# A conditioned attention and feed-forward block: token-major residual, crossbar transposes and resident output weights

## The chip, the cores and the metric

The kernel runs on one core of one Trainium2 chip. Times are device microseconds of that core. All times compared here are of runs in the fast state, beside runs of the kernel before on the same chip. The groups of runs ran on different chips; the kernel before took 1413.2 to 1414.2 us on each (median), so times are compared across groups too. Engines are named as in the profile: PE (TensorE matmuls), PEld (its weight loads), DVE (VectorE), ACT (ScalarE), POOL (GpSimd), SP (SyncE, which issues DMAs). In the kernels, SBUF tiles hold operands and PSUM banks (`ps`) the results of matmuls; a crossbar transpose is a DMA that transposes on its way (`dma_start_transpose`).

## The reference

```python
sa, ca, ga, sb, cb, gb = silu(c) @ w_mod            # six rows of 1024
h = layernorm(x) * (1 + ca) + sa                    # x: 2048 tokens x 1024
x = x + ga * attention(h)     # 32 query heads, 4 key heads, 512 cached keys, Dh 128, then @ wo (4096 x 1024)
h = layernorm(x) * (1 + cb) + sb
x = x + gb * ((silu(h @ w_gate) * (h @ w_up)) @ w_down)       # 3584 hidden columns
```

Both kernels work through chunks of 512 tokens. All four chunks pass attention and its output projection first, then all four pass the feed-forward. A chunk has 32 heads; a head costs 8 matmuls of 512 columns for the query, 4 for the scores, and 16 of 129 columns for probabilities times values (the last column sums the probabilities).

## The kernel before

The residual `xT` lies with features on partitions, so a layernorm sums over partitions. That is done on TensorE with a matrix of ones, twice a chunk and layernorm:

```python
for dt in range(DT):                                   # 8 matmuls; 8 more over the squares
    mm(bank(bS), ones_bf[:, :], xT[:, dt, chs], dt == 0, dt == DT - 1, ...)
```

Each normalised head is transposed on TensorE and copied out of PSUM by VectorE:

```python
def otr(i):
    for j in range(TPC):                               # 4 blocks of 128x128
        transpose(bb[:, j * P:(j + 1) * P], o_s[os_][:, j, :], [B_os[os_]], PB[TRB])
    T.op(DVE, lambda: V.tensor_copy(oT_all[:, h, :], bb[:, 0:CH]), ...)
```

The loop over heads (cut to its order); one pair of PSUM banks serves the whole down projection:

```python
for i in range(NA + 3):
    ...                         # query weights, 2 MB pieces of output weights, x tiles, late modulation
    qproj(i); scores(i - 1); pv(i - 2); otr(i - 3)
    if hD == Hq - 1: oproj_plain(chD)
    run_bg(...)                 # a step of a layernorm
DNB = [4, 5]                    # down projection: all pairs of output tiles use these two banks
```

Output weights are loaded again for each chunk. The later modulation rows come from 256 matmuls with one moving column. The result is transposed back on TensorE.

The softmax here doesn't subtract the row's maximum and nothing guards it: scores larger than these inputs give would overflow.

Of the kernel before, what the change touches and what calls it, by code (L numbers as in the profile page):

```python
# [3 lines left out]
ALU = mybir.AluOpType  # L4
AF = mybir.ActivationFunctionType
BF16 = mybir.dt.bfloat16
# [4 lines left out]
class _Stream:  # L11
    def __init__(self, name, sem, issuer, inc=1, self_exempt=False):
        self.name = name
        self.sem = sem
        self.issuer = issuer
        self.inc = inc
        self.count = 0
        self.self_exempt = self_exempt

# [20 lines left out]
class _Tracker:  # L40
    def __init__(self):
        self.issuer_synced = {}

    def stream(self, name, sem, issuer, inc=1, self_exempt=False):
        return _Stream(name, sem, issuer, inc, self_exempt)

    def _synced(self, st):
        key = id(st.issuer)
        d = self.issuer_synced.get(key)
        if d is None:  # L50
            d = {}
            self.issuer_synced[key] = d
        return d

    def op(self, st, emit, reads=(), writes=()):
        req = {}
        for b in reads:
            lw = b.last_write
            if lw is not None:
                s, c = lw  # L60
                if req.get(s, 0) < c:
                    req[s] = c
        for b in writes:
            lw = b.last_write
            if lw is not None:
                s, c = lw
                if req.get(s, 0) < c:
                    req[s] = c
            for s, c in b.reads.items():
                if req.get(s, 0) < c:  # L70
                    req[s] = c
        synced = self._synced(st)
        eng = st.issuer
        for s, c in req.items():
            if s is st and st.self_exempt:
                continue
            if synced.get(s, 0) >= c:
                continue
            eng.wait_ge(s.sem, c)
            synced[s] = c  # L80
        ins = emit()
        st.count += st.inc
        c = st.count
        ins.then_inc(st.sem, st.inc)
        for b in reads:
            b.reads[st] = c
        for b in writes:
            b.last_write = (st, c)
            b.reads = {}
        return c  # L90

    def wait_all(self, st, target):
        synced = self._synced(st)
        c = target.count
        if c > 0 and synced.get(target, 0) < c:
            st.issuer.wait_ge(target.sem, c)
            synced[target] = c


class _Arena:  # L100

    def __init__(self, tensor_ap, nbytes):
        self.t = tensor_ap
        self.nbytes = nbytes
        self.off = 0
        self.gen = 0
        self.regs = []

    def reset(self):
        self.off = 0  # L110
        self.gen += 1

    def take(self, shape_free, dtype, bufs):
        n = 1
        for s in shape_free:
            n *= s
        esz = 2 if dtype == BF16 else 4
        nb = n * esz
        nb_al = (nb + 63) // 64 * 64
        assert self.off + nb_al <= self.nbytes, "arena overflow"  # L120
        start, end = self.off, self.off + nb
        for (g, s0, e0, obufs) in self.regs:
            if g != self.gen and s0 < end and start < e0:
                for nbuf in bufs:
                    for ob in obufs:
                        nbuf.absorb(ob)
        self.regs.append((self.gen, start, end, list(bufs)))
        e0 = start // 2
        ap = self.t[:, e0:e0 + nb // 2]
        if dtype != BF16:  # L130
            ap = ap.bitcast(dtype)
        if len(shape_free) == 2:
            ap = ap.rearrange("p (a b) -> p a b", a=shape_free[0])
        elif len(shape_free) == 3:
            ap = ap.rearrange("p (a b c) -> p a b c", a=shape_free[0], b=shape_free[1])
        self.off += nb_al
        return ap


def bass_adaLN_cond__sliding_block_cached__swiglu_ffn__prompt_kernel(  # L140
# [16 lines left out]
    HD = A_wq.shape[1]  # L157
    Hq = HD // Dh
# [3 lines left out]
    assert Dh == P and D % P == 0 and S % 512 == 0 and W % P == 0  # L162
    DT = D // P
    ST = S // P
# [5 lines left out]
    NJ = 6 * DT  # L170
    assert NJ % 4 == 0 and Hq % 4 == 0 and FT % 4 == 0 and DT % 2 == 0 and Hq >= 8
    WMG = NJ // 4
    HG = Hq // 4
    FG = FT // 4
    GK = Hkv * KT
    assert GK <= 16
    att_scale = float(Dh) ** -0.5
    eps = 1e-5
    inv_d = 1.0 / float(D)
    NA = NCH * Hq  # L180
    NFI = NCH * FT
    DSTEPS = FT // 4
    assert DT // 2 * DSTEPS <= FT
    assert (DT // 2) * 8 <= Hq
# [5 lines left out]

    PE = T.stream("pe", nc.alloc_semaphore("s_pe"), nc.tensor, self_exempt=True)
    ACT = T.stream("act", nc.alloc_semaphore("s_act"), nc.scalar)
    DVE = T.stream("dve", nc.alloc_semaphore("s_dve"), nc.vector)
    POOL = T.stream("pool", nc.alloc_semaphore("s_pool"), nc.gpsimd)

    def dq(name, issuer=None):
        return T.stream(name, nc.alloc_semaphore(name), issuer or nc.sync, inc=16)

    S_ = lambda name, shape, dt: nc.alloc_sbuf_tensor(name, shape, dt)
    xT = S_("xT", [P, DT, S], BF16)  # L200
    hT = S_("hT", [P, DT, S], BF16)
    ident = S_("ident", [P, P], BF16)
    ones_bf = S_("ones_bf", [P, P], BF16)
    eps_col = S_("eps_col", [P, 1], F32)
    c6 = S_("c6", [P, NJ], F32)
    c6a = S_("c6a", [P, 2 * DT], F32)
    g1 = S_("g1", [P, DT], F32)
    g2 = S_("g2", [P, DT], F32)
    mod_bf = S_("mod_bf", [P, NJ], BF16)
    gtmp_bf = S_("gtmp_bf", [P, DT], BF16)  # L210
    cT_bf = S_("cT_bf", [P, DT], BF16)
    th_c = S_("th_c", [P, DT], F32)
    sg_c = S_("sg_c", [P, DT], F32)
    sc_bf = S_("sc_bf", [P, DT], BF16)
    rl = S_("rl", [P, 4], F32)
    xnat_t = S_("xnat", [P, 4, D], BF16)
    xnat = [xnat_t[:, i, :] for i in range(4)]
    ln_mean = S_("ln_mean", [P, CH], F32)
    ln_msq = S_("ln_msq", [P, CH], F32)
    ln_var = S_("ln_var", [P, CH], F32)  # L220
    ln_A = S_("ln_A", [P, CH], BF16)
    ln_B = S_("ln_B", [P, CH], BF16)
    NSQ = 8
    ln_sq = [S_("ln_sq%d" % i, [P, CH], BF16) for i in range(NSQ)]
    ln_t = [S_("ln_t%d" % i, [P, CH], BF16) for i in range(2)]
    ln_n = [S_("ln_n%d" % i, [P, CH], BF16) for i in range(2)]

    ARENA_BYTES = 108 * 1024
    arena_t = S_("arena", [P, ARENA_BYTES // 2], BF16)
    arena = _Arena(arena_t[:, :], ARENA_BYTES)  # L230

    ps_h = nc.alloc_psum_tensor("ps", [P, 4096], F32)
    ps = ps_h[:, :]
    ps_t = ps.tensor
# [7 lines left out]
    PB = [_Buf("bank%d" % b) for b in range(8)]  # L242

    B_xT = [[_Buf("xT_%d_%d" % (dt, ch)) for ch in range(NCH)] for dt in range(DT)]
    B_hT = [[_Buf("hT_%d_%d" % (dt, ch)) for ch in range(NCH)] for dt in range(DT)]
    B_ident = _Buf("ident"); B_ones = _Buf("ones"); B_eps = _Buf("eps")
    B_c6 = _Buf("c6"); B_c6a = _Buf("c6a"); B_g1 = _Buf("g1"); B_g2 = _Buf("g2")
    B_modbf = _Buf("modbf"); B_gtmp = _Buf("gtmp")
    B_cT = _Buf("cT"); B_thc = _Buf("thc"); B_sgc = _Buf("sgc"); B_sc = _Buf("sc")
    B_rl = _Buf("rl")  # L250
    B_xnat = [_Buf("xnat%d" % i) for i in range(4)]
    B_mean = _Buf("mean"); B_msq = _Buf("msq"); B_var = _Buf("var"); B_A = _Buf("A"); B_B = _Buf("B")
    B_sq = [_Buf("sq%d" % i) for i in range(NSQ)]
    B_lnt = [_Buf("lnt%d" % i) for i in range(2)]
    B_lnn = [_Buf("lnn%d" % i) for i in range(2)]

    Q_c = dq("q_c")
    Q_x = [dq("q_x%d" % i) for i in range(4)]
    Q_out = [dq("q_out%d" % i) for i in range(4)]

    QB = 4
    SCB = [0, 1, 2, 3]
    OA = 5
    OBT = 6
    TRB = 7
    OPB = 7
    OT_OFF = [0, 130, 260]
    MOD_EARLY_OFF = 0
    MOD_LATE_OFF = 400
    GB = [0, 1]  # L270
    UB = [2, 3]
    DNB = [4, 5]
    YTB = 6

    with nc.Block() as block:

        @block.gpsimd
        def _(g):
            V = nc.vector
            A = nc.scalar  # L280
            TE = nc.tensor
            SP = nc.sync

            def mm(out_ap, lhsT, rhs, start, stop, reads, bank_buf):
                T.op(PE, lambda: TE.matmul(out_ap, lhsT, rhs, start=start, stop=stop),  # L285
                     reads=reads, writes=[bank_buf])

            def transpose(out_ap, in_ap, reads, bank_buf):
                T.op(PE, lambda: TE.transpose(out_ap, in_ap, ident[:, :]),  # L289
                     reads=reads + [B_ident], writes=[bank_buf])  # L290
# [561 lines left out]
```

## Time and profile before

| | before |
|---|---|
| time, median of the first three runs | 1414.79 us |
| span of the profiled run | 1412.8 us |
| PE busy, share of span | 95% |
| DVE busy | 610.2 us |
| DMA moved | 178.53 MB |

These are lines of the profile's page of the kernel before: engines, the hardware DMA queue (packets, MB, share of 16 engines' time), and the chain of work that ended last.

```profile
span 1412.8 us, 20538 instructions
...
PE 1346.9 (95%) x8445; PEld 700.7 (50%) x8592; DVE 610.2 (43%) x1324; ACT 415.0 (29%) x674; POOL 59.4 (4%) x65
...
q1 hardware_dynamic: 237264, 177.22, 41.0%
...
PE 91%; DVE 3%; issue 2%; ACT 2%; SPq 2%; DMA 1%; DVEq 0%; ACTq 0%
...
L637 DVE COPY arena<-ps 128x512 bf16<-128x512 bf16 x128 | 53.1, 415 | 0.2 <-PE ps L289 0.2
L289 PE MATMUL ps<-ident,arena 128*128 128x128 bf16 x528 | 51.0, 221 | 1.4 <-DVE arena L637 1.4
```

The chain is 91% PE, so what counts is TensorE: work it need not do, and gaps between its matmuls. The mean of 221 ns for a transpose is a latency and not a cost, since matmuls overlap. A cost is read from start to start in the timeline: 216 ns for 512 columns, 59 for 129, 55 for a transpose. The busy share does not tell products from other work: 784 transposes and 128 sums over ones are inside those 95%.

The waits of PE in the kernel before (line waiting, what it waited for, total us, times, longest):

```profile
PE ps L285 <- DVE xT L776: 11.0, 24, 0.7
PE ps L289 <- DMA xnat<-in_A_x_dram: 7.6, 2, 4.7
PE ps L285 <- ACT hT L466: 6.4, 1, 6.4
PE ps L285 <- DVE arena L626: 6.4, 8, 1.0
PE ps L285 <- DVE arena L637: 6.2, 4, 1.7
```

L776 is the residual update of the down projection, L626 the scaling of a head, L637 the copy of a transposed head. The timeline of PE across a change of down columns shows what one of the first line's waits is (start, us, what, count, idle before it):

```profile
896.99 12.25 PE L285 MATMUL ps<-arena 128*128 128x512 bf16 x55
909.96 0.38 PE L285 MATMUL ps<-arena 128*128 128x512 bf16 x1 [0.72 <-DVE xT L776]
910.53 12.04 PE L285 MATMUL ps<-arena 128*128 128x512 bf16 x54 [0.19 <-DVE xT L776]
```

### The profile page before, as it was taken

Reading aid. Unit: us, or ns where it says so; the run is one execution under the profiler, and the core shown is the slowest. Engines: PE = TensorE matmul, PEld = TensorE weight load, DVE = VectorE, ACT = ScalarE, POOL = GpSimd, SP = SyncE. Lnnn points to the kernel's source line nnn. Section 1 sums busy time; section 2 is a strip of 40 time slices with the busy share of each in tenths; the row PEclk is TensorE's granted clock in tenths of the full one; section 3 lists DMA queues with packets and bytes.
Section 4 is the critical chain, followed back from the end, with each engine's and each line's share of the span. In section 5 each row is a group of like instructions: output and inputs, shape, how many; then the busy total and the mean of one; then the engine's idle time right before and its main releaser. Section 6 shows DMA issues by size and latency. Waiting matters only on the chain.

```text
span 1412.8 us, 20538 instructions
## 1 busy us (share of the span) xinstructions
PE 1346.9 (95%) x8445; PEld 700.7 (50%) x8592; DVE 610.2 (43%) x1324; ACT 415.0 (29%) x674; POOL 59.4 (4%) x65
## 2 busy tenths in 40 slices
PE   5989999999999999999999999999999999999998
PEld 3556644556545566455554444444443444444443
DVE  4566554656613566235671245313331333124311
ACT  4455540456503666025760021001110111001100
POOL 0220021000010000110001100000000000000000
PEclk7999999999999999999999999999999999999999
DMA  9663204522143421434204485308721683129410
GB/s 304 199 183 120 90 31 120 154 86 61 61 120 111 120 69 61 117 92 121 75 16 114 141 268 171 111 15 271 222 96 52 200 278 126 52 94 300 151 52 30
DMA packets 237357, 178.53 MB, mean 126 GB/s; under 512 B 7888, under 2 KB 233168, under 8 KB 237264
## 3 DMA queue, kind: packets, MB, share of 16 engines
q1 hardware_dynamic: 237264, 177.22, 41.0%
q8 instruction: 67, 1.10, 0.3%
q14 instruction: 26, 0.21, 0.1%
HBM read 173.02 MB, written 4.19 MB: 125 GB/s over the span
## 4 chain that ended last, share of the span: by engine, by line
PE 91%; DVE 3%; issue 2%; ACT 2%; SPq 2%; DMA 1%; DVEq 0%; ACTq 0%
PE ps L285 89%; PE ps L289 2%; ACT arena L603 1%; DVE xT L776 1%; DMA xnat<-in_A_x_dram 1%; DVE arena L626 1%; DVE rl L623 1%; SPq L526 0%; SPq L361 0%; ACT L603 0%; ACT L447 0%; DVE xnat L789 0%; SPq L530 0%; DVE ln_var L440 0%; DVE arena L628 0%
## 5 line engine op out<-in xcount | busy, mean ns | idle before, releaser
L285 PE MATMUL ps<-arena 128*128 128x512 bf16 (+1 forms) x4431 | 671.0, 306 | 17.4 <-DVE xT L776 11.0
L285 PE MATMUL ps<-hT,arena 128*128 128x512 bf16 x2724 | 618.6, 380 | 16.0 <-ACT hT L466 6.4
L285 PEld LDWEIGHTS ps<-arena 128*128 128x128 bf16 x4480 | 365.8, 98 | 339.3 <-issue 15.3
L285 PEld LDWEIGHTS ps<-hT,arena 128*128 128x128 bf16 x2816 | 270.5, 98 | 318.5 <-DMA arena<-in_A_wq_dram 6.3
L603 ACT ACTIVATE arena<-ps 128x512 bf16<-128x512 f32 x512 | 305.5, 597 | 347.0 <-PE ps L285 312.2
L756 ACT ACTIVATE arena<-ps 128x512 bf16<-128x512 f32 x112 | 66.9, 597 | 543.7 <-PE ps L285 543.7
L757 DVE SCALAR_TENSOR_TENSOR arena<-arena,ps 128x512 bf16<-128x512 bf16 x112 | 77.0, 688 | 173.5 <-ACT arena L756 173.5
L591 DVE CAST arena<-ps 128x512 bf16<-128x512 f32 x128 | 88.4, 690 | 49.8 <-PE ps L285 45.1
L776 DVE SCALAR_TENSOR_TENSOR xT<-ps,c,xT 128x512 bf16<-128x512 f32 x32 | 22.6, 747 | 183.2 <-PE ps L285 183.2
L760 DVE SCALAR_TENSOR_TENSOR arena<-arena,ps 128x512 bf16<-128x512 bf16 x112 | 77.0, 688 | 53.8 <-PE ps L285 53.7
L651 DVE SCALAR_TENSOR_TENSOR xT<-ps,c,xT 128x512 bf16<-128x512 f32 x32 | 24.0, 751 | 152.3 <-PE ps L285 152.1
L427 POOL TENSOR_TENSOR ln_sq<-xT 128x512 bf16<-128x512 bf16 x56 | 58.4, 1060 | 717.3 <-PE ps L285 671.8
L626 DVE TENSOR_TENSOR arena<-ps,rl 128x384 bf16<-128x384 f32 x128 | 71.4, 558 | 4.4
L622 DVE RECIPROCAL rl<-ps 128x3 f32<-128x3 f32 x128 | 23.1, 180 | 110.7 <-PE ps L285 110.7
L637 DVE COPY arena<-ps 128x512 bf16<-128x512 bf16 x128 | 53.1, 415 | 0.2 <-PE ps L289 0.2
L289 PE MATMUL ps<-ident,arena 128*128 128x128 bf16 x528 | 51.0, 221 | 1.4 <-DVE arena L637 1.4
L628 DVE TENSOR_SCALAR arena<-ps,rl 128x128 bf16<-128x128 f32 x128 | 44.9, 351 | 4.6
L289 PEld LDWEIGHTS ps<-ident,arena 128*128 128x128 bf16 x528 | 35.7, 98 | 1.6 <-DVE arena L637 1.6
L462 DVE TENSOR_TENSOR ln_n<-ln_t,ln_B 128x512 bf16<-128x512 bf16 x64 | 28.4, 444 | 1.2
L459 DVE TENSOR_TENSOR ln_t<-xT,ln_A 128x512 bf16<-128x512 bf16 x64 | 27.5, 430 | 0.0
L623 DVE RECIPROCAL rl<-ps 128x1 f32<-128x1 f32 x128 | 21.5, 168 | 13.6 <-PE ps L289 0.5
L285 PE MATMUL ps<-xT,ones_bf 128*128 128x512 bf16 x62 | 16.3, 410 | 4.0 <-DVE arena L637 3.0
(48 smaller groups left out, 207.6 us busy)
## 6 DMA issues: line engine op xcount, KB each, us to landing
arena<-in_A_wq_dram SPq DMA_DIRECT2D x32, 1024.0 KB, 5.4
arena<-in_A_wo_dram SPq DMA_DIRECT2D x16, 2048.0 KB, 10.7
arena<-in_B_w_gate_dram SPq DMA_DIRECT2D x28, 1024.0 KB, 5.2
arena<-in_B_w_up_dram SPq DMA_DIRECT2D x28, 1024.0 KB, 7.2
arena<-in_B_w_down_dram SPq DMA_DIRECT2D x16, 1792.0 KB, 11.8
hT<-in_w_mod_dram SPq DMA_DIRECT2D x8, 1024.0 KB, 9.4
xnat<-in_A_x_dram SPq DMA_DIRECT2D x16, 256.0 KB, 5.6
arena<-in_w_mod_dram SPq DMA_DIRECT2D x4, 1024.0 KB, 10.2
```

What stands on the lines that cost most here:

```text
L285: T.op(PE, lambda: TE.matmul(out_ap, lhsT, rhs, start=start, stop=stop), reads=reads, writes=[bank_buf])
L289: T.op(PE, lambda: TE.transpose(out_ap, in_ap, ident[:, :]), reads=reads + [B_ident], writes=[bank_buf])
L427: T.op(POOL, lambda: g.tensor_tensor(ln_sq[dt][:, :], xT[:, dt, chs], xT[:, dt, chs], ALU.mult), reads=[B_xT[dt][ch]], writes=[B_sq[dt]])
L591: T.op(DVE, lambda: V.tensor_copy(qT_s[qs], bank(QB)), writes=[PB[QB], B_qT[qs]])
L603: T.op(ACT, lambda: A.activation(ex_s[es][:, kt, :], bank(b), AF.Exp, scale=att_scale), writes=[PB[b], B_ex[es]])
L626: T.op(DVE, lambda: V.tensor_tensor(o_s[os_][:, 0:3, :], in3, rl3, ALU.mult), reads=[B_rl], writes=[PB[OA], B_os[os_]])
L628: T.op(DVE, lambda: V.tensor_scalar(o_s[os_][:, 3, :], bank(OBT, P, 0), rl[:, 3:4], None, op0=ALU.mult), reads=[B_rl], writes=[PB[OBT], B_ ...
L637: T.op(DVE, lambda: V.tensor_copy(oT_all[:, h, :], bb[:, 0:CH]), writes=[PB[TRB], B_oT[h]])
L756: T.op(ACT, lambda: A.activation(th_s[ts_], bank(gb), AF.Tanh, scale=0.5), writes=[PB[gb], B_th[ts_]])
L757: T.op(DVE, lambda: V.scalar_tensor_tensor(out=t1_s[ts_], in0=th_s[ts_], scalar=1.0, in1=bank(gb), op0=ALU.add, op1=ALU.mult), reads=[B_th ...
L760: T.op(DVE, lambda: V.scalar_tensor_tensor(out=guT[:, ft, :], in0=t1_s[ts_], scalar=0.5, in1=bank(ub), op0=ALU.mult, op1=ALU.mult), reads= ...
L776: T.op(DVE, lambda: V.scalar_tensor_tensor(out=xT[:, dtile, chs], in0=bank(DNB[dcol]), scalar=c6[:, 5 * DT + dtile:5 * DT + dtile + 1], in ...
```

## The change

The intent is to take from TensorE all that is not a product, and to leave VectorE lighter. The residual becomes token-major, so statistics are a VectorE instruction along the free dimension (`bn_stats`). Normalised tiles and heads are transposed by DMA through the crossbar. Output weights (8 MB) and later the down weights stay in SBUF. The later modulation is summed on VectorE from loaded rows. One flat map of SBUF replaces pools. The core of the diff, with cuts:

```diff
-for dt in range(DT):
-    mm(bank(bS), ones_bf[:, :], xT[:, dt, chs], dt == 0, dt == DT - 1, ...)
+for hf in range(2):
+    T.op(DVE, lambda: V.bn_stats(st_sb[i][:, 6*hf:6*hf+6], x_sb[:, t, 512*hf:512*hf+512]), ...)
 ...
-    transpose(bb[:, j * P:(j + 1) * P], o_s[os_][:, j, :], [B_os[os_]], PB[TRB])
-T.op(DVE, lambda: V.tensor_copy(oT_all[:, h, :], bb[:, 0:CH]), ...)
+T.op(tr_queue(), lambda: SP.dma_start_transpose(oT[:, h, :]..., o_sb[i % NOS]),
+     reads=[B_os[i % NOS]], writes=[B_oT[h]])
 ...
-load_wo(0) ... load_wo(3)            # every chunk, 2 MB each
+if ch == 0 and h % 2 == 0 and 8 <= h < 8 + 2 * NWO:
+    load_wo((h - 8) // 2)            # once, 8 pieces of 1 MB
 ...
-mm(bank(b, 1, off), ap[:, kc, jj*P:(jj+1)*P], sc_bf[:, kc:kc+1], ...)     # later modulation
+for kc in range(1, DT):
+    if kc % 2: yield                 # two products in a step
+    T.op(DVE, lambda: V.scalar_tensor_tensor(acc, ms[:, kc, :], sc[:, kc:kc+1], acc, op0=ALU.mult, op1=ALU.add), ...)
 ...
-DNB = [4, 5]
+b = 4 + dn[0] % 4                    # down projection: four banks in turn
+NQ, NEX, NOS = 4, 2, 2               # NOS: buffers for normalised heads
```

## The prediction

> **What bounds the kernel now.** TensorE: the page puts 91% of the chain that ended last on PE. In the timeline a 128x512 matmul starts every 216 ns, a 128x129 one every 59, a 128x128 transpose every 55, a one-column modulation matmul every 25. The Trainium skill ("TensorE: Matmul & The Clock Gate", Back-to-back issue gap) gives N/2.4 + 2.5 ns, 216 at 512 and 56 at 129; the trace agrees at 512.
>
> Both kernels need 5248 matmuls of 512 columns (1133.6 us) and 2048 of 129 (120.8 us): 1254.4 us. The other 158 us of the 1412.8 us span are overhead:
> - PE work beyond the products: 784 transposes (43 us), 128 layernorm sums (27.6), 384 modulation matmuls (9.6).
> - The head: full speed only from 35 us (timeline); less the one projection done by then, 33 us.
> - PE waits: 11.0 us for the residual update of down columns, about 19 us for normalised heads and layernorm statistics; a tail of 7 us.
>
> **What the change does.** PE loses 512 head transposes (28 us), 128 output transposes (7), 96 of x (5), the layernorm sums (27.6) and 256 late modulation matmuls (6.4, and 6.4 of waits). It gains 16 broadcasts and small sums: 2.5 us. Down's waits (11 us) go, since four banks rotate. VectorE work per head falls from 2.36 us to about 1.57 (cast 0.69, reciprocal 0.18, scaling estimated 0.70), against 3.54 us on PE (12 x 216 + 16 x 59 ns).
>
> **New costs, estimated.**
> - Head: 4 MB of modulation weights still come first (landed at 18.5 us in before, 2.75 us per MB); scaling takes 8 x 0.41 us, query weights land near 21 us. First projection at 20.5 us; with single-bank copies and key transposes, 24.5 us beyond the products.
> - The queue. Transposes, loads and stores share SyncE. In heads 8 to 23 of chunk 0, resident output weights, query weights, x and modulation ask for 310 to 380 GB/s, about before's best rate. Heads' transposes stand behind 1 MB loads with only two head buffers: 10 us of stall.
> - VectorE: a modulation step (1.4 us) and statistics (1.3) in one head exceed the roughly 1.9 us spare: 6 us.
> - Attention to output projection and back (last head's transpose, one bank's copy): 10 us.
> - Tail: a 256-column block, two VectorE steps, a store (2.0 us to landing in before): 3 us.
>
> Sum: 1254.4 + 24.5 + 2.5 + 10 + 6 + 10 + 3 = 1310 us; waits overlap a little: 1307 us.
>
> **What would show it.** 128x512 matmuls still 216 ns apart; on PE no layernorm sums and 49 transposes. First projection near 20 us. Steady head 3.54 us instead of 3.75. Later chunks' attention near 115 us (before: 131, 126, 118). Feed-forward with its output projection near 645 us instead of 671. Chunk 0 keeps most waits, on DMA-released head buffers or on VectorE.
>
> **What would make it wrong.** A crossbar transpose of 128x512 is the one operation no trace here shows. The Trainium skill ("VectorE: DVE Perf Modes", The three transpose paths) gives 1309 ns for 128x128; I estimate 3 to 4 us to landing, and under 1.7 us of issue on SyncE. If issuing takes over 3 us, SyncE paces attention and most of the gain is lost; if transposes slow the loads, chunk 0 stalls. If resident weights come late, the first output projection waits. If stalls hide entirely: 1285 us.
>
> Predicted 1307 us, 1286 to 1340 eight times in ten; faster by over 2%: 0.94, within 2%: 0.04, slower: 0.02.

## The result, and the profile after

The changed kernel took 1308.82 us (median of 4 runs, 1305.2 to 1310.57) beside 1414.2 us. The ratio is 0.9253, 95% interval 0.9237 to 0.9269. A ratio is the mean time of one kernel's fast runs over that of the other's of the same rounds, so it is not quite the ratio of the medians quoted. The prediction was 1307 us.

The same lines of the page, after:

```profile
span 1307.7 us, 18541 instructions
...
PE 1274.6 (97%) x7553; PEld 643.2 (49%) x7553; DVE 561.6 (43%) x1058; ACT 336.6 (26%) x630; POOL 19.6 (1%) x41
...
q1 hardware_dynamic: 217744, 154.57, 45.8%
...
PE 90%; DMA 6%; DVE 4%; issue 0%; SPq 0%; DVEq 0%
...
L260 PE MATMUL ps<-arena 128*128 128x128 bf16 (+1 forms) x49 | 5.4, 278 | 3.6 <-DVE arena L325 3.6
```

Transposes on TensorE fell to 49. DMA, 1% of the chain before, is now 6%. The queue moves 13% fewer bytes yet takes a larger share of the engines. The waits of PE after:

```profile
PE ps L256 <- DVE arena L472: 9.6, 8, 2.3
PE ps L256 <- DVE arena L494: 6.2, 6, 2.3
PE ps L256 <- DMA arena<-in_w_mod_dram: 5.0, 2, 4.3
...
PE ps L256 <- DVE arena L504: 3.2, 4, 0.9
```

L472 casts the query out of PSUM, L494 scales a head, L504 is the residual update. No wait is left on layernorm sums or copied transposes, and the feed-forward has none: the chain holds one unbroken piece of PE there, 580.4 us long.

```profile
724.65 580.40 PE ps L256 x2716
```

Two sums made from the trace's start times are used below. *Gaps*: for each matmul, the time to the next start beyond the usual one, where it exceeds 0.15 us and a record is not merely missing. From the first steady matmul on they come to 28.7 us after, of which 4.2 us are matmuls that ran at half rate right behind a stall. *Attention of a chunk*: from its first to its last 129-column matmul. (In the kernel before the first head of chunk 1 comes ahead of chunk 0's output projection, and so on, so that its stretches hold 33, 32, 32 and 31 heads.) Two profiles of the changed kernel, this one and the control below, differ in these stretches by 0.7, 2.2, 0.3 and 0.9 us; a smaller difference between single profiles shows nothing.

| | before | after |
|---|---|---|
| attention of chunks 0 to 3, us | 153.9, 123.5, 123.4, 117.0 | 122.0, 117.5, 113.4, 106.7 |
| last output projection and feed-forward, us | 670.6 | 639.7 |
| first query projection starts, us | 28.3 | 20.8 |

### The profile page after: what moved, and what is told of

Read it like the earlier page. It is cut to its first block, busy times and chain, and to the rows that moved or that the text cites. A ratio compares the mean times of both kernels' runs of the same rounds, so it can differ in the third digit from the quotient of the medians.

```text
span 1307.7 us, 18541 instructions
## 1 busy us (share of the span) xinstructions
PE 1274.6 (97%) x7553; PEld 643.2 (49%) x7553; DVE 561.6 (43%) x1058; ACT 336.6 (26%) x630; POOL 19.6 (1%) x41
## 3 DMA queue, kind: packets, MB, share of 16 engines
HBM read 125.83 MB, written 4.19 MB: 99 GB/s over the span
## 4 chain that ended last, share of the span: by engine, by line
PE 90%; DMA 6%; DVE 4%; issue 0%; SPq 0%; DVEq 0%
PE ps L256 90%; DMA arena<-arena 5%; DVE arena L494 1%; DVE arena L472 1%; DVE arena L533 1%; DMA arena<-in_w_mod_dram 1%; DVE arena L337 0%; PE ps L260 0%; DVE arena L504 0%; DVE arena L359 0%; SPq L266 0%; DVE arena L493 0%; DVE arena L539 0%; SPq L273 0%; DVE arena L538 0%
## 5 line engine op out<-in xcount | busy, mean ns | idle before, releaser
L256 PE MATMUL ps<-arena 128*128 128x512 bf16 (+2 forms) x7504 | 1270.8, 331 | 26.9 <-DVE arena L472 9.6
L256 PEld LDWEIGHTS ps<-arena 128*128 128x128 bf16 x7504 | 639.1, 98 | 657.3 <-issue 15.1
L479 ACT ACTIVATE arena<-ps 128x512 bf16<-128x512 f32 x512 | 264.1, 604 | 385.1 <-PE ps L256 385.1
L681 ACT ACTIVATE arena<-ps 128x512 bf16<-128x512 f32 x112 | 66.9, 597 | 522.9 <-PE ps L256 522.9
L504 DVE TENSOR_TENSOR arena<-ps,arena 128x512 bf16<-128x512 f32 (+1 forms) x65 | 44.4, 683 | 341.2 <-PE ps L256 341.2
L472 DVE CAST arena<-ps 128x512 bf16<-128x512 f32 x128 | 87.9, 687 | 46.3 <-PE ps L256 45.8
L494 DVE TENSOR_TENSOR arena<-ps,arena 128x512 bf16<-128x512 f32 x128 | 88.5, 692 | 35.3 <-DMA arena<-arena 31.9
L493 DVE RECIPROCAL arena<-ps 128x4 f32<-128x4 f32 x128 | 23.3, 182 | 106.6 <-PE ps L256 106.3
L337 DVE BATCH_NORM_STATS2 arena<-arena 128x6 f32<-128x512 bf16 x64 | 44.2, 690 | 1.1
L533 DVE SCALAR_TENSOR_TENSOR arena<-arena 128x512 f32<-128x512 bf16 x56 | 41.8, 746 | 0.8
L506 DVE TENSOR_TENSOR arena<-arena 128x512 bf16<-128x512 bf16 (+1 forms) x65 | 27.4, 421 | 2.2
L359 DVE TENSOR_SCALAR arena<-arena 128x512 bf16<-128x512 bf16 x64 | 23.1, 407 | 0.1
```

The source lines that it names most:

```text
L256: T.op(PE, lambda: TE.matmul(out_ap, lhsT, rhs, start=start, stop=stop, skip_group_check=loose), reads=reads, writes=[bb])
L337: T.op(DVE, lambda: V.bn_stats(st_sb[i][:, 6 * hf:6 * hf + 6], x_sb[:, t, 512 * hf:512 * hf + 512]), reads=[BX[t]], writes=[B_st[i]])
L472: T.op(DVE, lambda: V.tensor_copy(q_sb[i % NQ], bank(QBK)), writes=[PB[QBK], B_q[i % NQ]])
L479: T.op(ACT, lambda: A.activation(ex[i % NEX][:, kt, :], bank(SCB[kt]), AF.Exp, scale=att_scale), writes=[PB[SCB[kt]], B_ex[i % NEX][kt]])
L493: T.op(DVE, lambda: V.reciprocal(rl, den), writes=both + [B_rl])
L494: T.op(DVE, lambda: V.tensor_tensor(o_sb[i % NOS].rearrange("p (a b) -> p a b", a=TPC), num, rl_bc, ALU.mult), reads=[B_rl], writes=both + ...
```

## The experiments

All ran beside the kernel before on one chip per group. Edits are against the changed kernel unless said otherwise. The two theories at first: Q, the remaining waits come from crossbar transposes that land late and so free a head's buffer late; V, they come from steps of modulation and statistics that overload VectorE.

**Control.** No edit.

> The changed kernel itself, unaltered, as a control for the three runs beside it. Expected by every theory: 1308 us, ratio to the kernel before 0.925, and in its trace again about 32 us of VectorE idle in front of the head scaling, ended by a DMA, and about 25 us of TensorE waits after the first steady matmul.

Measured: 1307.43 us, ratio 0.9252 (0.9239 to 0.9265); gaps 26.3 us. The VectorE timeline at the first long stall (start, us, instruction, idle before it):

```profile
73.42 0.17 DVE L493 RECIPROCAL arena<-ps 128x4 f32<-128x4 f32 x1
77.77 0.69 DVE L494 TENSOR_TENSOR arena<-ps,arena 128x512 bf16<-128x512 f32 x1 [4.18 <-DMA arena<-arena]
```

The scaling waits 4.18 us for a transpose to have read the buffer it wants to write. SyncE's timeline shows what that transpose stood behind:

```profile
67.35 1.10 SPq L525 DMA_DIRECT2D arena<-in_w_mod_dram  x1
68.50 0.59 SPq L266 DMA_DIRECT2D arena<-in_A_x_dram  x1
69.14 0.45 SPq L451 DMA_DIRECT2D arena<-in_A_wo_dram  x1
69.69 1.51 SPq L500 DMA_TRANSPOSE arena<-arena  x1
```

The 1 MB piece of output weights (L451) landed at 77.31 us by the trace, the transpose (L500) at 77.68, 8 us after its issue began. With nothing ahead, a transpose lands 2.4 us after its issue begins, of which 1.19 us is the issue itself; the median of all 159 in this run (28 of them of layernorm tiles, 128x1024) is 3.8 us. In the whole run VectorE's scaling waited so:

```profile
DVE arena L494 <- DMA arena<-arena: 29.8, 28, 4.2
```

**Four head buffers.**

```diff
-NQ, NEX, NOS = 4, 2, 2
+NQ, NEX, NOS = 3, 2, 4      # a query buffer and the warm-up tile give the room
```

> Four buffers for normalised heads instead of two; nothing else moves (query buffers go from four to three, which the order of work allows). Theory Q (TensorE's interior waits come from crossbar transposes that stand behind 1 MB loads in one queue, so that the head scaling waits for its buffer): VectorE idle ended by a DMA in front of the head scaling falls from 32 to under 3 us, transposes still take as long to land, TensorE waits in the first two chunks fall from about 19 to under 9 us, time falls by 8 to 14 us, to about 1297. Theory V (the waits come from modulation and statistics steps that overload VectorE, DMA waits being hidden): time within 3 us of the control.

Measured: 1291.87 us, ratio 0.9141 (0.9128 to 0.9153), 15.6 us less than the control. Chunk 0's attention fell from 122.7 to 112.5 us and all gaps from 26.3 to 12.3. Transposes land as late as before (median 3.8 us), but the scaling no longer waits for one. The timeline at the same place:

```profile
73.27 0.18 DVE L495 RECIPROCAL arena<-ps 128x4 f32<-128x4 f32 x1 [0.67 <-PE ps L257]
73.48 0.69 DVE L496 TENSOR_TENSOR arena<-ps,arena 128x512 bf16<-128x512 f32 x1
```

Theory Q holds as far as the late buffer goes, and more was saved than it named. Whether the transposes are late because of the order in the queue or because the DMA engines are full, this run does not tell.

**Slim modulation.** Wrong result on purpose: only two of eight products are summed.

```diff
 for kc in range(1, DT):
     if kc % 2: yield
+    if kc > 1: continue
```

> The later modulation sums only two of its eight products on VectorE (the result is wrong on purpose; loads, broadcasts and order stay). Theory V: time falls by 8 to 14 us, to about 1297. Theory Q: VectorE idle ended by a DMA stays near 32 us and the time falls by less than 4 us. If both are needed for a stall (a late buffer and then a long step), each of the two runs removes more than half of it and the two savings add up to more than the whole.

Measured: 1299.31 us, ratio 0.9198 (0.9185 to 0.921), 8.1 us less than the control; gaps 18.9 us. VectorE still waits for DMAs:

```profile
DVE arena L494 <- DMA arena<-arena: 33.2, 31, 3.8
```

So V is partly true as well. The sign that a stall needs both did not come: slim modulation removed less than half of the 26.3 us of gaps, and the two savings add up to 23.7 us, not to more than the whole. Stall by stall, start to start, the three traces show three kinds. One at 75.9 us in the control (2.36 us) stays with slim modulation and goes with four buffers: the buffer alone. Three at 50, 232 and 417 us (1.0 to 1.1 us) stay with four buffers, and with slim modulation go or fall to 0.3: the steps alone. Others give way to either, such as the one at 89.3 us (2.45 us; 1.0 with slim modulation, 0.9 with four buffers): there a late buffer puts the VectorE queue behind, and long steps keep it there until TensorE stops. The first profile of the changed kernel shows the same stall, on VectorE and then on PE; the query cast (L472) that TensorE needs comes after the late scaling, a modulation step (L533) and a statistics step (L337):

```profile
88.11 0.69 DVE L494 TENSOR_TENSOR arena<-ps,arena 128x512 bf16<-128x512 f32 x1 [2.56 <-DMA arena<-arena]
88.72 1.53 DVE L533 SCALAR_TENSOR_TENSOR arena<-arena 128x512 f32<-128x512 bf16 x2
90.16 1.42 DVE L337 BATCH_NORM_STATS2 arena<-arena 128x6 f32<-128x512 bf16 x2
91.49 0.67 DVE L472 CAST arena<-ps 128x512 bf16<-128x512 f32 x1
...
92.22 5.99 PE L256 MATMUL ps<-arena 128*128 128x512 bf16 x31 [2.29 <-DVE arena L472]
```

**Heads transposed on TensorE again.**

```diff
-T.op(tr_queue(), lambda: SP.dma_start_transpose(oT[:, h, :]..., o_sb[i % NOS]), ...)
+for j in range(TPC):
+    transpose(bank_bf(XBK)[:, j*P:(j+1)*P], o_sb[i % NOS][:, j*P:(j+1)*P], P, [B_os[i % NOS]], PB[XBK])
+T.op(DVE, lambda: V.tensor_copy(oT[:, h, :], bank_bf(XBK)[:, 0:CH]), writes=[PB[XBK], B_oT[h]])
```

> Undo one part: the heads are transposed on TensorE again (four transposes a head and one VectorE copy of 0.42 us), no crossbar transposes of heads. TensorE's own work grows by 512 x 55 ns = 28 us. Theory P (TensorE bounds, the crossbar's waits are small change): time grows by 20 to 28 us, to about 1330, since part of the waits of 32 us on transposes goes away. Rival X (the crossbar gave back what it saved): time within 8 us of the control, 1308 to 1316.

Measured: 1339.37 us, ratio 0.9477 (0.9464 to 0.9489), 31.9 us more than the control. That is above Theory P's range and refutes X. The copies out of one bank bring new waits of PE (L502 is the copy):

```profile
PE ps L256 <- DVE arena L502: 12.6, 12, 1.5
...
PE ps L260 <- DVE arena L502: 4.4, 4, 1.1
```

**Loads from ScalarE's queue.** Query weights, output weights, x and modulation of the attention stage; transposes stay on SyncE's queue.

```diff
-T.op(Q_wo[i], lambda: SP.dma_start(...), ...)       # and Q_x, Q_wq, Q_ms
+T.op(on(Q_wo[i]), lambda: LQ[0].dma_start(...), ...)   # LQ[0] is ScalarE from the first qproj on
```

> The changed kernel with the loads of the attention stage (query weights, output weights, x, modulation) issued from ScalarE's queue; crossbar transposes stay alone on SyncE's; still two head buffers. Theory Q-order (a transpose is late because it stands in line behind loads): transposes land about 2.4 us after issue even beside loads, VectorE idle ended by a DMA in front of the head scaling falls from 30 to under 8 us, time falls by 8 to 16 us against the control's ratio of 0.925, if ScalarE bears the issuing. Rival Q-load (the 16 engines are simply full in the first chunk): landing times in the first chunk stay at 4 to 8 us and the time stays within 4 us of the control.

Measured: 1309.43 us, ratio 0.926 (0.9244 to 0.9276): no gain. By chunk the attention took 126.4, 113.1, 111.7 and 105.9 us, against the control's 122.7, 115.3, 113.1 and 105.8. VectorE's waits in front of the scaling:

```profile
DVE arena L500 <- DMA arena<-arena: 19.5, 12, 5.2
```

Fewer waits than in the control (29.8 us, 28 times), but longer ones. Over the first 140 us the median landing time of the transposes rose from 5.0 to 6.3 us. So there the rival is right, the engines are full (DMA share 0.95 from 60 to 100 us, 1.01 in the control). In chunks 1 and 2 the attention is 2.2 and 1.4 us shorter, but chunk 1 differs by 2.2 us between two profiles of one kernel too, so a saving by the second queue is not shown. That chunk 0 does not gain fits what the Trainium skill says in "DMA: Bandwidth & Descriptors", Issuing engines are not separate DMA queues: transfers started by different engines run on the same 16 DMA engines and interleave. Why chunk 0 became worse was not tested apart.

**All three fixes.** Four buffers; the banks of the output projection swapped; one modulation product a step beside a layernorm task (and the first feed-forward layernorm queued two heads later, to let the modulation finish).

```diff
-b = [XBK, QBK][k % 2]                 # output projection: its last block ended in the query's bank
+b = [QBK, XBK][k % 2]
-    if kc % 2:
+    if kc % 2 or len(tasks) > 1:
         yield
-if ch == NCH - 1 and h == 2:          # first feed-forward layernorm
+if ch == NCH - 1 and h == 4:
```

> Four head buffers, the two banks of the output projection swapped (so that the last block does not end in the bank that the next query projection needs), and one modulation product a step instead of two while a layernorm task runs beside it. Expected from the four-buffer run's trace: its 12 us of interior TensorE waits lose the four waits of 0.95 us and most of the waits on query casts, down to 4 to 6 us; time about 1285 us, ratio 0.909. If the steps are not what delays the casts, only the 3.8 us of the banks go: 1288 us.

Measured: 1283.38 us, ratio 0.9078 (0.9064 to 0.9091), correct. That is 24.1 us less than the control and beats both kernels. Gaps 4.8 us. No run splits the 8.5 us beyond four buffers between the other two edits; the waits give hints. The bank swap removed the waits on the residual update, and those on the query cast fell to these:

```profile
PE ps L257 <- DVE arena L474: 1.5, 5, 0.8
```

**Crossbar transposes alone, in the kernel before.**

```diff
-    transpose(bb[:, j * P:(j + 1) * P], o_s[os_][:, j, :], ...)      # and the VectorE copy
+T.op(Q_tr[i % 4], lambda: SP.dma_start_transpose(oT_all[:, h, :]..., o_s[os_]...), ...)
```

> One part alone, in the kernel before: the heads are transposed by the crossbar instead of TensorE, all else as it was. TensorE's work falls by 28 us and VectorE's by 53. Theory P (transposes on TensorE cost their full time): time falls by 25 to 36 us, to about 1382. Rival X (two head buffers and loads of 2 MB ahead in the queue eat it): falls by less than 15 us.

Measured: 1397.44 us, ratio 0.9882 (0.9859 to 0.9905), 15.9 us less than before. It lies between the two expectations. Attention of chunks 1 to 3 lost 3.8, 4.8 and 4.3 us, chunk 0 only 1.5, where 7.0 us of TensorE work each (128 x 55 ns) were removed.

**The same with four head buffers.**

```diff
-NQT = 3; NEX = 2; NOS = 2
+NQT = 3; NEX = 2; NOS = 4
```

> The kernel before with crossbar transposes of heads, as in the run before_xbar, and four head buffers instead of two. Theory B (the part alone gave 16 us instead of 28 mostly because a head buffer is freed late): VectorE idle ended by a DMA in front of the head scaling goes from 12.6 us to under 2, and the time falls by 22 to 28 us against the kernel before, to about 1388. Rival (the loss is elsewhere: x tiles later, the waits on normalised heads that modulation matmuls have anyway): within 3 us of the run with two buffers, about 1396.

Measured: 1387.49 us, ratio 0.9816 (0.9803 to 0.983), 25.8 us less than before. Theory B holds. In the run with two buffers VectorE waited as follows; with four there is no such wait.

```profile
DVE arena L627 <- DMA arena<-arena: 12.6, 4, 3.8
```

**Rotating down banks alone, in the kernel before.**

```diff
-DNB = [4, 5]
+DNB = [[4, 5], [6, 7]]                # pair pp % 2
```

> One part alone, in the kernel before: the down projection's accumulators alternate between two pairs of banks instead of one pair. Expected by the prediction's account: of the 11.0 us of TensorE waits on the residual update most go, time falls by 8 to 11 us, to about 1404, ratio 0.993. Rival: the wait moves to the output transposes, which share those banks, and the time falls by less than 4 us.

Measured: 1398.37 us, ratio 0.9891 (0.9876 to 0.9906), about 15 us less, above the expected 8 to 11. The 11.0 us wait is gone, and the one that the rival named did not grow (2.5 us, 2.9 before):

```profile
PE ps L289 <- DVE xT L776: 2.5, 4, 0.6
```

The surplus was in the reading. The view counts idle time from the modelled end of a matmul (0.38 us after its start) while the next could have started after 0.216 us. Each wait thus costs 0.16 us more than shown. Start to start, the 24 waits of the kernel before come to 14.8 us, which is what the run saved.

**Layernorm's share of TensorE put back.** 112 unused matmuls of 512 columns, four a tile in 28 layernorm tiles.

```diff
 ln_rstd(i)
+for k in range(4):
+    mm(bank(EXTRA[0]), ident, x_sb[:, t, 0:512], k == 0, k == 3, ...)
```

> The changed kernel with 112 matmuls of 512 columns added to its 28 later layernorm tiles (four a tile; results unused), as many as the old layernorm sums of these chunks had on TensorE. Theory P (TensorE bounds): time grows by 112 x 216 ns = 24 us against the control, to about 1331. Rival (the layernorm's place on TensorE or VectorE does not matter since waits absorb it): grows by less than 12 us.

Measured: 1326.04 us, ratio 0.9381 (0.9366 to 0.9397), 18.6 us more than the control. 77% of the 24.2 us of added work (112 x 216 ns) arrived. The gaps fell from 26.3 to about 21 us, nearly all of it in chunk 0 (12.0 to 7.6), so the rest went into what had been waits. Theory P holds in kind: TensorE bounds, but part of the new work fills stalls.

**Output weights spread over more heads.**

```diff
-if h % 2 == 0 and 8 <= h < 8 + 2 * NWO: load_wo((h - 8) // 2)
+if h % 3 == 2 and 8 <= h < 8 + 3 * NWO: load_wo((h - 8) // 3)
```

> The changed kernel with the eight loads of resident output weights issued every third head (8 to 29) instead of every second (8 to 22); two head buffers as in the control. Theory Q-load (in the first chunk the engines are full, so transposes land late whatever queue the loads use): first chunk's attention falls from 122.7 us by 4 to 8 us, later chunks as in the control, time about 1302. Rival Q-order (what matters is one load directly in front of a transpose, however many there are): within 2 us of the control.

Measured: 1305.6 us (1302.86 to 1308.88), ratio 0.9235 (0.9217 to 0.9253). Chunk 0's attention fell by 4.2 us as expected of Q-load, but chunk 1's grew by 3.0, little more than two profiles of the changed kernel differ there (2.2). The time is 1.8 us from the control, not clear of it and inside the range of Q-order, so this run does not decide between the two.

## Why the prediction was right

**What bounds.** TensorE did. The terms of products and removed work were nearly right: 512 columns still take 216 ns, 49 transposes remain. A 129-column matmul takes 57 ns and not 59, so the products (1254.4 us) were 4 us too high (2048 x 2 ns). Put alone into the kernel before, transposes and bank rotation gave 25.8 us (with enough buffers) and about 15; put back into the changed kernel, 112 of the layernorm matmuls cost 18.6. No run tests alone what the transposes of x and of the result, the later modulation and the head gave. By stage the forecast holds as well: in the stretches that the prediction used (131, 126 and 118 us before) the later chunks' attention took 121, 116 and 110 us, predicted near 115, and the last output projection with the feed-forward 639.7, predicted near 645.

**Head and tail.** First projection predicted at 20.5 us, measured 20.8. Time beyond the products predicted 24.5 us, measured 23.4 (the third projection starts at 26.83 us, less two of 1.73). Tail 3 us, measured 2.9 from the last matmul's start. One reading of the kernel before was off: full speed did not come at 35 us, since the granted clock was still 0.50 from 35 to 40 us and 1.00 from 40 to 45.

**The stalls.** The sum of 26 us was met by 26.3 to 28.7 us. Its split was not, and that the sum fits is luck: one term was 6 us too large, the other two together 6 to 9 us too small.
- Between attention and output projection 10 us were predicted. The gap view shows four waits of about 1 us on one bank, 3.9 us together, and no wait on the last head's transpose. This term was oversized by 6 us.
- Queue (10) and VectorE (6) were too small: without the 3.9 us of the bank, 22.4 to 24.8 us of gaps are left for them. Four buffers alone saved 15.6 us and slim modulation alone 8.1; some stalls had one cause, some both, so the two amounts are not cleanly separate either.
- The queue argument said that transposes stand behind loads. They do in the queue, but moving the loads to another queue gained nothing. In chunk 0 the full engines count (DMA share 1.01 from 60 to 100 us, at 275 GB/s), as the demand of 310 to 380 GB/s had suggested.
- The half-rate matmuls behind stalls were not predicted; they are 4.2 us of the 28.7.

**The crossbar.** Predicted under 1.7 us of issue and 3 to 4 us to landing for 128x512; measured 1.19 us, and a median of 3.5 us over the transposes of heads (4.0 with those of layernorm tiles). The Trainium skill's 1309 ns for 128x128 ("VectorE: DVE Perf Modes", The three transpose paths) is for another size, so no run here checks it.

**Resident weights.** HBM reads fell from 173.02 to 125.83 MB. Loading 8 MB within chunk 0 is probably part of why its engines are full: spreading the pieces took 4.2 us off that chunk in one profile. No run isolates a gain from residency.

## What to carry to other kernels

When TensorE bounds, work can move from it to DMA. Here that brought nearly the whole saving (25.8 us of 28) only when the buffers covered the longest times to landing, not the usual one; two more buffers of 1 KB a partition were worth 16 us. Read the cost of a wait from start to start, since the view of waits understated each one, by 0.16 us behind a 512-column matmul here. When two causes of stalls meet on one engine, test each alone and follow single stalls through the traces: a sum that fits, as here, says nothing of its terms.

## What the Trainium skill lacked or had wrong

- "Advanced Engine Details and Errata" (X-Bar Transpose (TRN2)) says "TRN2 transpose DMAs are as fast as regular DMAs", and "DMA: Bandwidth & Descriptors" (Latency and other measured facts) gives 261 GB/s, or about 350 to 400 when contiguous. Here crossbar transposes within SBUF were slower. In the control's DMA records, packets under 512 B (105,895, nearly all of transposes; before had 7,895) carried 25.1 MB and took 192 us of the 16 engines' time, 130 GB/s, while packets of 512 to 1024 B ran at 318. Hence a larger share with fewer bytes. Part of this is crowding: a head's transpose with nothing beside it had its packets (544, 131 KB) under way for 0.91 us, 144 GB/s, and by the packets' own time ran at 202. Whether the transposing or the small packets make it slow is not separated; the kernel before, without such transposes, moved its 7,895 small packets at 156.
- "DMA: Bandwidth & Descriptors" gives sequencer cycles of a transpose for other sizes only. Measured for 128x512 within SBUF, issued by SyncE: 1.19 us of issue, 2.4 us from its begin to landing with nothing ahead.
- "TensorE: Matmul & The Clock Gate" (Why this matters for your kernels; also the two states of Part 1) advises no idle gaps above about 3 us, since the clock drops after an idle window of about 3.4 us. Here shorter ones were enough. In the control the granted clock was half from 91.0 to 97.8 us, behind two stalls of 2.3 us with 1.1 us of matmuls between. In the first profile of the changed kernel it was half from 79.8 to 83.2 us, behind a single stall of 2.3 us that ended at 78.8; a like stall of 2.2 us in the control, ended at 78.5, left it at 1.00. The windows of the control (stretch, length, busy time per engine, granted clock, DMA share, GB/s):

```profile
89.00:92.00 3.00, 0.71 (x10) 0.46 (x8) 2.90 (x7) 0.00 (x0) 0.00 (x0) 0.83 1.02 274
92.00:95.00 3.00, 3.00 (x8) 1.06 (x7) 2.24 (x5) 0.00 (x0) 0.55 (x1) 0.50 0.30 61
```

- No page read for this case gives a duration of `bn_stats`: 690 ns for 128x512 bf16 in this trace.
